# Which engines read the late copy of the test's sum, and which queue stores two of the last row blocks

## The chip, the cores and the metric

The kernel runs on one core of a Trainium2 chip. The metric is the device time of one execution in microseconds. The core has five engines with a sequencer each: TensorE (PE; its weight loads are shown as PEld), VectorE (DVE), ScalarE (ACT), GpSimd (POOL) and SyncE (SP). A sequencer issues its engine's instructions in their order, waits on semaphores, branches, and can issue DMAs. In this kernel SyncE, ScalarE and GpSimd issue DMAs, each on a queue of its own.

## The reference

An attention with a sliding window of 128 keys and 4 "sink" keys is followed by a gated block with a residual. All is float32; B = 4, H = 8, S = 768, D = 64, so rows of 512.

```python
scores = scale * np.matmul(q, k.transpose(0, 1, 3, 2))
keep = is_sink | in_window
scores = np.where(keep, scores, -1000000000.0)
scores = scores - np.max(scores, axis=-1, keepdims=True)
a = np.exp(scores)
a = a / (np.sum(a, axis=-1, keepdims=True) + 1e-09)
x = np.matmul(a, v)                      # heads joined to (4, 768, 512)
...
h = gelu_tanh(x @ w_in)                  # 512 -> 1024, split into u and v
v_n = (v - mu) / np.sqrt(var + 1e-06) * g_ln
v_s = np.einsum('ts,bsd->btd', w_sg, v_n) + b_sg[None, :, None]
return x + (u * v_s) @ w_out
```

## The kernel before, in words

The kernel works on 16 pairs of heads (4 batches of 4 pairs) and, per batch, on one block of the gated part. For a pair it loads k, q and v, brings k and q to columns, computes the scores only where the window or the sinks let through, takes exp without the maximum, multiplies by v with a column of ones for the denominator, and scales. For a batch it computes the two halves of the hidden layer, normalises v, multiplies by `w_sg`, gates, and projects with `w_out`. The result of a batch leaves in six blocks of 128 rows: a matmul group (`pj`), an addition of the residual on VectorE (`o`, line 918) and a store to the result (`store`, line 928).

Nothing is scheduled at run time. Every step is an `Op` with a name; a list of names, `FIRST`, gives the order in which all steps are written out, and so the order of each engine's own instructions. The buffers `o_sb` hold a row block from the addition until its store has landed.

The batch 3 blocks end the kernel. They are written in the order 2 (`pj32`), 1, 0, 3, 4, 5, and then a block of batch 2 in two halves of 256 columns, `pj23x` and `pj23y` (`LAST = (2, 3)`, chosen to come at the end). Stores go on SyncE's queue, but for the second half, `store23y`, which goes on ScalarE's.

Leaving out the maximum is right only while no denominator is out of range. So there is a test: GpSimd compares all reciprocals with two bounds (`compare`), TensorE adds up the ones (`tally`), VectorE reduces them to one integer, `total` (`summed`, lines 1112 and 1114). At the end, `with tc.If(found["total"] < COUNT)` (line 1306) branches: every engine compares the value in its own register, and when the sum is full it jumps over `general()`, a second, slow version of the whole computation. For this, every engine must load the sum from memory to a register (`ask`, line 1126, a TENSOR_LOAD in the profile).

Five engines do so at different places. SyncE loads `total` in the step `peek`, ScalarE in `peek_act`. VectorE, TensorE and GpSimd load a copy of it: the step `copied` (line 1140) writes `total` into the first column of the buffer of row block `MARK = (3, 4)`, which it may do only when that block's store has landed, since the store reads that buffer. The step `look` then loads from there. Behind the branch comes the end of the program (line 1338): GpSimd settles the semaphores of its own DMA queue, SyncE waits for all semaphores in turn, and a barrier joins the engines.

Of the kernel before, what the change touches and what calls it, by code (L numbers as in the profile page):

```python
# [9 lines left out]
I32 = mybir.dt.int32  # L10
# [39 lines left out]
class Planner:  # L50
# [15 lines left out]
    def add(self, *args, **kwargs):  # L66
        op = Op(*args, **kwargs)
        self.ops.append(op)
        return op
# [86 lines left out]
    "look"  # L156
)
TAKERS = (
    "zero_a0:ACT zero_a1:DVE zero_a2:DVE zero_a3:DVE low_a:DVE zero_b0:DVE zero_b1:DVE "
# [19 lines left out]
def kernel(  # L179
# [14 lines left out]
    nc = tc.nc  # L194

    B, H, S, Dh = q.shape
# [33 lines left out]
        o_sb=([128, DM], F32), st=([128, 6], F32))  # L230
# [5 lines left out]
    def bank(shape, dtype, name, buf=None):  # L236
        if buf is not None and buf.room is R["s"]:
            return ps_s.tile(shape, dtype, name=name, tag="s")
        return ps_m.tile(shape, dtype, name=name, tag="m")

    T = {}
    add = plan.add
# [10 lines left out]
    WARM = 8  # L253
    AHEAD = (0, 1)
    LAST = (2, 3)
    MARK = (B - 1, 4)
    LONG = ()
    BY_DMA = (11,12,13,14,15)
    W_DMA = ()
# [21 lines left out]
    total = consts.tile([128, 1], I32, name="total")  # L281
# [53 lines left out]
    def make_mask(m, at):  # L335
        for h in range(2):
# [6 lines left out]
                    rank=-2000)  # L343
    T["dark0"] = add("dark0", {"DVE": 450}, lambda _: make_dark0(), [T["dark"]], use=[dark],
                     rank=-1998)
# [5 lines left out]
    if LONG:  # L351
        T["spread"] = add("spread", {"POOL": 900}, lambda _: make_spread(), new=[spread],
                          rank=-378)
# [83 lines left out]
    def pos(n):  # L437
        return divmod(n, HP)
# [451 lines left out]
    def project(b, t, rank, rooms):  # L890
        ps = Buf([R[r] for r in rooms])
        o_sb = Buf([R["k_f"], R["q_f"], R["o_sb"]] if b == B - 1 else R["o_sb"])
        gT, x = T["gT", b], T["x", b]

        halves = [slice(0, DM)] if (b, t) != LAST else \
            [slice(0, DM // 2), slice(DM // 2, DM)]
        for i, cols in enumerate(halves):
            whole, w = len(halves) == 1, cols.stop - cols.start
            if i:
                ps = Buf([R[r] for r in rooms])  # L900
                o_sb = Buf(o_sb.rooms)
            tail = "" if whole else "xy"[i]

            def emit(_, ps=ps, cols=cols, w=w):
                ps.tile = bank([128, 512], F32, "o_ps", ps)
                for c in range(KU):
                    nc.tensor.matmul(ps.tile[:, 0:w], gT.tile[:, c, 128 * t:128 * (t + 1)],  # L907
                                     w_out_sb[:, c, cols], start=(c == 0), stop=(c == KU - 1))

            T["pj", b, t] = a = add(f"pj{b}{t}{tail}", {"PE": 865 if whole else 435}, emit,  # L910
                    [T["gT_", b, f, t // HT] for f in range(KU)] + [T["w_out"]],
                    new=[ps], use=[gT, x], rank=rank)

            def leave(_, ps=ps, o_sb=o_sb, cols=cols, w=w):
                tag = o_sb.room.name
                o_sb.tile = work.tile([128, DM], F32, name="o_sb", tag=tag, bufs=R[tag].size)
                heads = slice(cols.start // 128, cols.stop // 128)
                nc.vector.tensor_add(  # L918
                    o_sb.tile[:, 0:w].rearrange("p (h d) -> p h d", d=128),
                    ps.tile[:, 0:w].rearrange("p (h d) -> p h d", d=128),  # L920
                    x.tile[:, heads, t, :])

            a = add(f"o{b}{t}{tail}", {"DVE": 690 if whole else 380}, leave, [a], new=[o_sb],
                    use=[ps, x], rank=rank - 2000)

            def store(_, o_sb=o_sb, cols=cols, w=w, i=i):
                queue = nc.scalar if i else nc.sync
                queue.dma_start(out=out[b, 128 * t:128 * (t + 1), cols],
                                in_=o_sb.tile[:, 0:w])

            T["o_sb", b, t] = o_sb
            T["st", b, t] = add(f"store{b}{t}{tail}", {"ACT" if i else "SP": 380}, store, [a],
                                use=[o_sb], rank=-50, move=800 if whole else 400, lag=300)


# [76 lines left out]
    def turn_g(_):  # L1012
# [4 lines left out]
    a = add("turn_g", {"PE": 330}, turn_g, [T["g_row"], T["one"]], new=[g_ps], use=[g_row],  # L1017
            rank=9000)
# [20 lines left out]
    def block(b, rank, gate):  # L1039

        ahead = [T[("sc", *g)] for g in gate]
        gate = [T[("exp", *g)] for g in gate]
        cols = [T["xc", HP * b + hp] for hp in range(HP)] + ahead
        got = [hidden_v(b, j, rank + 0.1 * j, cols, gate) for j in range(NT)]
        for m in range(2):
            normalise(b, list(range(HT * m, HT * (m + 1))), rank + 0.05)
        got += [hidden_u(b, f, m, rank + 1 + 0.1 * f + m, cols, gate)
                for m in range(2) for f in range(KU)]
        rooms = ["m", "s"] if b == B - 1 else ["m"]
        for m in range(2):  # L1050
            for f in range(KU):
                spatial(b, f, m, 10000 + 1000 * b + 10 * (KU * m + f), rooms)
        for t in range(NT):
            project(b, t, 10500 + 1000 * b + 10 * t, rooms)
        return got

    gate = []
    for n in range(NP):
        r = 100 * n
        b, hp = pos(n)  # L1060
# [25 lines left out]
    COUNT = 2 * 128 * NP * NT * 2  # L1086
    flat = rcps.rearrange("p n c i h o -> p (n c i h o)")

    def compare(_):
# [8 lines left out]
    a = add("compare", {"POOL": 900}, compare,  # L1098
            [T["rcp", n, c] for n in range(NP) for c in range(2)],
            new=[fits], rank=12000)  # L1100
# [8 lines left out]
    a = add("tally", {"PE": 180}, tally, [a], new=[ps], use=[fits], rank=12900)  # L1109
# [6 lines left out]
    a = add("summed", {"DVE": 500}, summed, [a], use=[ps], rank=12900)  # L1116
    found = {}
# [2 lines left out]
              mybir.EngineType.SP]  # L1120

    WHY = "a sum of so many zeros and ones"
    ASKED = [mybir.EngineType.SP, mybir.EngineType.Activation]

    def ask(tile, engines):
        return nc.values_load(tile[0:1, 0:1], engines=engines, min_val=0, max_val=COUNT,
                              skip_runtime_bounds_check_because=WHY)

    def peek(_):
        found["SP"] = ask(total, ASKED[0:1])

    def peek_act(_):
        found["ACT"] = ask(total, ASKED[1:2])

    held_o = T["o_sb", *MARK]

# [2 lines left out]

    def look(_):
        tc.mark_branch_hint_location("rest", HINT, engines=HINTED)
        rest = ask(held_o.tile[:, 0:1].bitcast(I32), [e for e in mybir.ALL_ENGINES if e not in ASKED])
        found["total"] = type(rest).of_register_unchecked(
            type(rest.val)([*found["SP"].val, *found["ACT"].val, *rest.val]), min_val=0,
            max_val=COUNT)

    for part in segments:
        for lead, follow in zip(part[0::2], part[1::2]):  # L1150
# [2 lines left out]
            follow.rank = plan.first.get(follow.name, -10000)  # L1153
    for t in range(NT):
        T["pj", B - 1, t].behind.append(a)
    add("peek", {"SP": 750}, peek, [a], rank=0)
    add("peek_act", {"ACT": 750}, peek_act, [a], rank=0)
    T["st", -1, 0] = add("copied", {"DVE": 150}, copied, [a, T["st", *MARK]], use=[held_o],
                         rank=0)
    add("look", {"SP": 1200}, look, [a, T["st", -1, 0]] + [T["st", B - 1, t] for t in range(NT)], rank=0)  # L1160
    plan.run()

# [180 lines left out]
```

## Time and profile before

| what | value |
|---|---|
| three runs | 162.88, 165.15, 162.61 us; median 162.88 |
| the profiled execution | 162.92 us |
| its span, first to last instruction | 160.9 us |
| granted TensorE clock, mean | 0.998 |
| busy: PE, DVE, ACT, POOL | 94%, 82%, 67%, 52% of the span |
| DMA | 32.42 MB, 201 GB/s over the span |
| read from HBM, written | 24.81 MB, 6.29 MB |

The profile is of one execution, whose own time of 162.92 us is 2.0 us more than its span: what comes before the first and after the last instruction belongs to an execution too. Times in the views count from the start of the span. Names are those of the program: `out_dram<-o_sb` is a store of a row block, `o_sb<-o_ps,x` the addition before it, `o_sb<-total` the late copy, `<-total` and `<-o_sb` at line 1126 the loads to a register. An engine's name with a q behind it (SPq, POOLq) is its sequencer, whose instructions don't count as busy. The view of one line lists, for each kind of instruction, how many there were, their minimum, median and maximum duration in ns, and the first and the last start in us.

### The profile page before, as it was taken

How to read it: one execution, taken by the hardware profiler on the slowest of the kernel's cores; microseconds unless marked ns; L12 is line 12 of the kernel's file. 1: busy time of each engine (PE TensorE's matmuls, PEld its weight loads, DVE VectorE, ACT ScalarE, POOL GpSimd, SP SyncE). 2: the span in 40 equal slices, each digit the busy share in tenths (PEclk: the TensorE clock that was granted, in tenths of full speed). 3: DMA queues.
4: the chain of work that ended last, by engine and by line, in shares of the span. 5: the costliest groups of instructions: out<-in, count | busy, mean ns of one | idle time of the engine just before them, and what ended most of it. 6: DMA issues, size and time to landing. Idle time of an engine off the chain costs nothing.

```text
span 160.9 us, 4016 instructions
## 1 busy us (share of the span) xinstructions
PE 151.2 (94%) x1562; PEld 87.7 (55%) x1562; DVE 132.3 (82%) x283; ACT 107.6 (67%) x143; POOL 83.5 (52%) x126
## 2 busy tenths in 40 slices
PE   6899999999999999999799999998999999999960
PEld 2454574667657576456555664545556545555530
DVE  7556887798897999789999989589999969888960
ACT  6198787897979797979686875747995187701100
POOL 3645944155899695287957743573779403200000
PEclk9999999999999999999999999999999999999999
DMA  4999999998999956999876879799966330130182
GB/s 152 332 247 311 194 169 201 203 304 265 344 306 295 275 143 182 328 238 259 141 218 154 194 188 257 131 297 256 215 172 175 114 130 0 65 134 0 65 322 82
DMA packets 67877, 32.42 MB, mean 201 GB/s; under 512 B 56564, under 2 KB 64772, under 8 KB 67856
## 3 DMA queue, kind: packets, MB, share of 16 engines
q1 hardware_dynamic: 65328, 29.26, 70.1%
q0 software_dynamic: 2384, 2.75, 10.6%
q8 instruction: 13, 0.21, 0.6%
q10 hardware_dynamic: 144, 0.13, 0.2%
q14 instruction: 8, 0.07, 0.1%
HBM read 24.81 MB, written 6.29 MB: 193 GB/s over the span
## 4 chain that ended last, share of the span: by engine, by line
PE 79%; DVE 8%; POOL 4%; DMA 4%; ACT 1%; issue 1%; SPq 0%; DVEq 0%; POOLq 0%; ACTq 0%
PE vs L864 20%; PE hv L751 11%; PE o_ps L907 11%; PE hu L793 10%; PE sc L610 9%; PE av L676 8%; PE cps L550 4%; PE sc L590 3%; DMA q_f<-in_q_dram 2%; DVE vn L840 2%; PE xps L726 2%; POOL mv L820 2%; DVE o_sb L918 2%; DMA out_dram<-o_sb 2%; DVE mv L826 1%; DVE ex L638 1%
## 5 line engine op out<-in xcount | busy, mean ns | idle before, releaser
L627 ACT ACTIVATE ex<-sc 128x1024 bf16<-128x1024 f32 x48 | 47.4, 1024 | 9.7 <-PE sc L610 9.6
L864 PE MATMUL vs<-wsgT,vn 128*128 128x384 bf16 x192 | 35.5, 326 | 1.4 <-DVE vn L840 1.1
L864 PEld LDWEIGHTS <-vn 128*128 128x128 bf16 x192 | 17.5, 98 | 13.1 <-DVE vn L840 1.5
L793 PE MATMUL hu<-xT,w_in_sb 128*128 128x384 bf16 x128 | 23.6, 326 | 0.8 <-DVE o_sb L918 0.8
L801 ACT ACTIVATE uT<-hu 128x384 bf16<-128x384 f32 x32 | 14.9, 489 | 12.3 <-PE hu L793 12.1
L907 PE MATMUL o_ps<-w_out_sb,gT 128*128 128x512 bf16 (+1 forms) x100 | 23.1, 371 | 0.0
L751 PE MATMUL hv<-w_in_sb,xT 128*128 128x512 bf16 x96 | 22.5, 379 | 0.0
L875 DVE SCALAR_TENSOR_TENSOR vs<-vs,g_sb,b_bc 128x384 f32<-128x384 f32 x32 | 19.6, 621 | 2.8 <-PE vs L864 1.2
L773 DVE BATCH_NORM_STATS2 st<-v_all 128x6 f32<-128x512 f32 x24 | 16.3, 677 | 6.3 <-ACT v_all L762 6.3
L249 POOL CAST cast<-k_f 128x768 bf16<-128x768 f32 x16 | 13.7, 858 | 14.1 <-DMA k_f<-in_k_dram 12.8
L610 PE MATMUL sc<-qT,kT 64*128 64x256 bf16 (+2 forms) x320 | 18.9, 249 | 0.4 <-ACT qT L247 0.4
L311 POOL TENSOR_SCALAR_AFFINE_SELECT ex<-ex 128x512 bf16<-128x512 bf16 (+1 forms) x23 | 15.1, 655 | 7.9 <-ACT ex L627 7.7
L676 PEld LDWEIGHTS <-ex 128*128 128x128 bf16 x480 | 16.7, 97 | 4.1 <-issue 1.4
L695 DVE TENSOR_TENSOR x<-av,rcps 128x384 bf16<-128x384 f32 x32 | 17.5, 552 | 0.9
L883 DVE TENSOR_TENSOR gT<-vs,uT 128x384 bf16<-128x384 f32 x32 | 17.5, 556 | 0.9
L676 PE MATMUL av<-v_sb,ex 128*128 128x65 bf16 x352 | 18.0, 194 | 0.1
L249 POOL CAST cast<-q_f 128x768 bf16<-128x768 f32 x15 | 13.1, 872 | 9.7 <-issue 4.6
L793 PEld LDWEIGHTS <-w_in_sb 128*128 128x128 bf16 x128 | 12.3, 98 | 9.7 <-issue 1.2
L918 DVE TENSOR_TENSOR o_sb<-o_ps,x 128x512 f32<-128x512 f32 (+1 forms) x25 | 16.2, 663 | 1.3 <-PE o_ps L907 1.2
L762 ACT ACTIVATE v_all<-hv 128x512 f32<-128x512 f32 x24 | 13.7, 598 | 5.2 <-PE hv L751 5.0
L249 POOL CAST v_sb<-v_f 128x768 bf16<-128x768 f32 x16 | 13.9, 869 | 2.3 <-DMA v_f<-in_v_dram 2.3
L751 PEld LDWEIGHTS <-xT 128*128 128x128 bf16 x96 | 9.2, 98 | 10.5 <-DVE xT L249 0.6
(71 smaller groups left out, 197.6 us busy)
## 6 DMA issues: line engine op xcount, KB each, us to landing
k_f<-in_k_dram SPq DMA_DIRECT2D x16, 384.0 KB, 5.9
q_f<-in_q_dram SPq DMA_DIRECT2D x16, 384.0 KB, 5.1
v_f<-in_v_dram SPq DMA_DIRECT2D x16, 384.0 KB, 5.9
out_dram<-o_sb SPq DMA_DIRECT2D x23, 256.0 KB, 2.2
wsg<-in_moe_w_sg_dram POOLq DMA_DIRECT2D x2, 576.0 KB, 10.5
w_in_sb<-in_moe_w_in_dram POOLq DMA_DIRECT2D x2, 512.0 KB, 7.6
w_out_sb<-in_moe_w_out_dram POOLq DMA_DIRECT2D x1, 512.0 KB, 7.8
b_bc<-in_moe_b_sg_dram SPq DMA_DIRECT2D x1, 384.0 KB
```

Of the source, the lines that this page charges most:

```text
L249: eng[e].tensor_copy(dst, src)
L610: nc.tensor.matmul(sc.tile[row:row + keys, h, col:col + m], kT.tile[rows, k0:k0 + keys], qT.tile[rows, q0:q0 + m], start=not by_pe, stop=n ...
L627: nc.scalar.activation(out=ex.tile, in_=sc.tile, func=AF.Exp, scale=scale)
L676: nc.tensor.matmul(av.tile[:, m, h, :], ex.tile[:, h, col:col + 128], val, start=first, stop=(m == HT - 1 and h == 1 and at == len(steps) ...
L695: nc.vector.tensor_mul(x.tile[:, hp, HT * c:HT * (c + 1), :].rearrange("p i (h d) -> p i h d", h=2), av.tile[:, :, :, 0:64], rcp.to_broadc ...
L751: nc.tensor.matmul(ps.tile[:, 0:512], xT.tile[:, c, 128 * j:128 * (j + 1)], w_in_sb[:, c, DF:], start=(c == 0), stop=(c == KD - 1))
L793: nc.tensor.matmul(ps.tile[:, 0:NH], w_in_sb[:, c, 128 * f:128 * (f + 1)], xT.tile[:, c, NH * m:NH * (m + 1)], start=(c == 0), stop=(c == ...
L864: nc.tensor.matmul(ps.tile[:, 0:NH], vn.tile[:, si, 128 * f:128 * (f + 1)], wsgT[:, si, cols], start=(si == 0), stop=(si == NT - 1))
L875: nc.vector.scalar_tensor_tensor(out=ps.tile[:, 0:NH], in0=ps.tile[:, 0:NH], scalar=g_sb[:, f:f + 1], in1=b_bc[:, cols], op0=ALU.mult, op1 ...
L883: nc.vector.tensor_mul(gT.tile[:, f, cols], ps.tile[:, 0:NH], uT.tile[:, f, cols])
L907: nc.tensor.matmul(ps.tile[:, 0:w], gT.tile[:, c, 128 * t:128 * (t + 1)], w_out_sb[:, c, cols], start=(c == 0), stop=(c == KU - 1))
L918: nc.vector.tensor_add(o_sb.tile[:, 0:w].rearrange("p (h d) -> p h d", d=128), ps.tile[:, 0:w].rearrange("p (h d) -> p h d", d=128), x.til ...
```

## The change

GpSimd and VectorE no longer load the late copy but `total` itself, in steps of their own, `peek_POOL` and `peek_DVE`. TensorE is the only engine left that loads the copy. The copy goes into the buffer of row block 3 in place of row block 4, and so it waits for that block's store. The stores of row blocks 3 and 5 of batch 3 go on ScalarE's queue. Line numbers of the changed kernel are up to three higher.

```diff
-    "gT301 hu331 gelu_u331 peek_act store32 gT331 pj31 o31 store31 pj30 o30 store30 pj33 o33 "
-    "store33 pj34 o34 store34 pj35 o35 store35 pj23x o23x store23x pj23y o23y store23y copied "
-    "look"
+    "gT301 hu331 gelu_u331 peek_POOL store32 gT331 pj31 o31 store31 pj30 o30 store30 pj33 "
+    "peek_ACT o33 store33 pj34 o34 store34 pj35 o35 store35 pj23x o23x store23x pj23y o23y "
+    "store23y peek_DVE copied look"
...
-    MARK = (B - 1, 4)
+    BY_ACT = {(B - 1, 3), (B - 1, 5)}
+    MARK = (B - 1, 3)
...
+            by = "ACT" if i or (b, t) in BY_ACT else "SP"
+
-            def store(_, o_sb=o_sb, cols=cols, w=w, i=i):
-                queue = nc.scalar if i else nc.sync
+            def store(_, o_sb=o_sb, cols=cols, w=w, by=by):
+                queue = nc.scalar if by == "ACT" else nc.sync
...
-    ASKED = [mybir.EngineType.SP, mybir.EngineType.Activation]
+    EARLY = dict(SP=mybir.EngineType.SP, ACT=mybir.EngineType.Activation,
+                 POOL=mybir.EngineType.Pool, DVE=mybir.EngineType.DVE)
...
-    def peek(_):
-        found["SP"] = ask(total, ASKED[0:1])
-
-    def peek_act(_):
-        found["ACT"] = ask(total, ASKED[1:2])
+    def peek(e):
+        found[e] = ask(total, [EARLY[e]])
...
-        rest = ask(held_o.tile[:, 0:1].bitcast(I32), [e for e in mybir.ALL_ENGINES if e not in ASKED])
+        rest = ask(held_o.tile[:, 0:1].bitcast(I32),
+                   [e for e in mybir.ALL_ENGINES if e not in EARLY.values()])
...
-    add("peek_act", {"ACT": 750}, peek_act, [a], rank=0)
+    for e in EARLY:
+        add("peek" if e == "SP" else f"peek_{e}", {e: 100 if e == "DVE" else 750}, peek, [a], rank=0)
```

On GpSimd, behind its last arithmetic (the second normalisation of batch 3), stood the load of the late copy; a name's number is that of its buffer, and `o_sb_2753` is row block 4:

```order
L818 TENSOR_SCALAR mv_2497<-mv_2497 128x3 [waits DVE_49]
L820 TENSOR_TENSOR mv_2497<-mv_2497,half_72 128x3 [waits Pool_49]
L818 TENSOR_SCALAR mv_2497<-mv_2497 128x3 [waits DVE_49]
L820 TENSOR_TENSOR mv_2497<-mv_2497,half_72 128x3 [waits Pool_49]
L1126 TENSOR_LOAD o_sb_2753 [waits DVE_49]
L1306 COMPARE_AND_BRANCH
```

Now the load at the same place takes `total`:

```order
L819 TENSOR_SCALAR mv_2497<-mv_2497 128x3 [waits DVE_49]
L821 TENSOR_TENSOR mv_2497<-mv_2497,half_72 128x3 [waits Pool_49]
L819 TENSOR_SCALAR mv_2497<-mv_2497 128x3 [waits DVE_49]
L821 TENSOR_TENSOR mv_2497<-mv_2497,half_72 128x3 [waits Pool_49]
L1130 TENSOR_LOAD total_90 [waits DVE_49]
L1308 COMPARE_AND_BRANCH
```

The wait is for VectorE both times: before for the late copy, now for `total`. On VectorE, the end of the program before was this; `o_sb_2745`, `_2753` and `_2761` are row blocks 3, 4 and 5, `_2769` and `_2777` the two halves, and a wait on DMAHW is one for the landing of a DMA:

```order
L918 TENSOR_TENSOR o_sb_2753<-o_ps_2748,x_2132 128x512 [waits DMAHW6_49,PE_49]
L918 TENSOR_TENSOR o_sb_2761<-o_ps_2756,x_2132 128x512 [waits DMAHW7_49,DVE_49,PE_49]
L918 TENSOR_TENSOR o_sb_2769<-o_ps_2764,x_1545 128x256 [waits DMAHW2_49,PE_49]
L918 TENSOR_TENSOR o_sb_2777<-o_ps_2772,x_1545 128x256 [waits DMAHW3_49,PE_49]
L1140 COPY o_sb_2753<-total_90 128x1 [waits DMAHW2_49,DVE_49]
L1126 TENSOR_LOAD o_sb_2753 [waits DVE_49]
L1306 COMPARE_AND_BRANCH
```

Now it is this, with row block 3 in `o_sb_2748`:

```order
L919 TENSOR_TENSOR o_sb_2756<-o_ps_2751,x_2132 128x512 [waits DMAHW6_49,PE_49]
L919 TENSOR_TENSOR o_sb_2764<-o_ps_2759,x_2132 128x512 [waits DMAHW7_49,DVE_49,PE_49]
L919 TENSOR_TENSOR o_sb_2772<-o_ps_2767,x_1545 128x256 [waits DMAHW2_49,PE_49]
L919 TENSOR_TENSOR o_sb_2780<-o_ps_2775,x_1545 128x256 [waits DMAHW3_49,PE_49]
L1130 TENSOR_LOAD total_90 [waits DVE_49]
L1141 COPY o_sb_2748<-total_90 128x1 [waits DMAHW1_49,DVE_49]
L1308 COMPARE_AND_BRANCH
```

VectorE's load moved ahead of the copy, and the copy waits for another store. On ScalarE, the end before was:

```order
L801 ACTIVATE uT_2542<-hu_2672 128x384 [waits PE_49]
L801 ACTIVATE uT_2542<-hu_2713 128x384 [waits PE_49]
L1126 TENSOR_LOAD total_90 [waits DVE_49]
L928 DMA out_0_dram<-o_sb_2777 128x256 [waits DMAHW4_49,DVE_49]
L1306 COMPARE_AND_BRANCH
```

And now:

```order
L802 ACTIVATE uT_2542<-hu_2713 128x384 [waits PE_49]
L1130 TENSOR_LOAD total_90 [waits DVE_49]
L931 DMA out_0_dram<-o_sb_2748 128x512 [waits DMAHW1_49,DVE_49]
L931 DMA out_0_dram<-o_sb_2764 128x512 [waits DMAHW3_49,DVE_49]
L931 DMA out_0_dram<-o_sb_2780 128x256 [waits DMAHW5_49,DVE_49]
L1308 COMPARE_AND_BRANCH
```

Row blocks 3 and 5 came onto ScalarE's queue ahead of the last half, and left SyncE's. Each store there stands behind a wait for its addition and for an earlier DMA. TensorE's order is the same as before, but for the buffer that its load reads. No other instruction of the path past the branch is moved.

More of the change, by code (lines that the diff above doesn't have):

```diff
@@ L931, in project @@
             T["o_sb", b, t] = o_sb
-            T["st", b, t] = add(f"store{b}{t}{tail}", {"ACT" if i else "SP": 380}, store, [a],
+            T["st", b, t] = add(f"store{b}{t}{tail}", {by: 380}, store, [a],
                                 use=[o_sb], rank=-50, move=800 if whole else 400, lag=300)
@@ L1143, in look @@
         tc.mark_branch_hint_location("rest", HINT, engines=HINTED)
-        rest = ask(held_o.tile[:, 0:1].bitcast(I32), [e for e in mybir.ALL_ENGINES if e not in ASKED])
-        found["total"] = type(rest).of_register_unchecked(
-            type(rest.val)([*found["SP"].val, *found["ACT"].val, *rest.val]), min_val=0,
-            max_val=COUNT)
+        rest = ask(held_o.tile[:, 0:1].bitcast(I32),
+                   [e for e in mybir.ALL_ENGINES if e not in EARLY.values()])
+        regs = [r for e in EARLY for r in found[e].val] + list(rest.val)
+        found["total"] = type(rest).of_register_unchecked(type(rest.val)(regs), min_val=0,
+                                                          max_val=COUNT)
     for part in segments:
@@ L1155 @@
         T["pj", B - 1, t].behind.append(a)
-    add("peek", {"SP": 750}, peek, [a], rank=0)
-    add("peek_act", {"ACT": 750}, peek_act, [a], rank=0)
+    for e in EARLY:
+        add("peek" if e == "SP" else f"peek_{e}", {e: 100 if e == "DVE" else 750}, peek, [a], rank=0)
     T["st", -1, 0] = add("copied", {"DVE": 150}, copied, [a, T["st", *MARK]], use=[held_o],
```

## The prediction, made before the run

> **What bounds the kernel now.** I read the page first: its busy shares, and TensorE's row of the 40 slices, of 4.0 us each.
>
> ```profile
> span 160.9 us, 4016 instructions
> PE 151.2 (94%) x1562; PEld 87.7 (55%) x1562; DVE 132.3 (82%) x283; ACT 107.6 (67%) x143; POOL 83.5 (52%) x126
> PE   6899999999999999999799999998999999999960
> ```
>
> TensorE is at work in nearly every slice, so up to about 156 us it sets the time. The change touches no matmul and nothing that a matmul waits for; it lies in the last two digits, 6 and 0. So I turned to the end of the chain of waits, and to the busy time of all engines in three stretches of the tail (their columns: length, then busy time of PE, PEld, DVE, ACT and POOL, the clock, the share of the DMA engines, GB/s).
>
> ```profile
> 150.33 3.47 PE o_ps L907 x16
> 153.82 0.70 DVE o_sb L918
> 154.54 2.72 DMA out_dram<-o_sb
> 157.35 0.15 DVE o_sb L1140
> ...
> 156.10:157.30 1.20, 0.00 (x0) 0.00 (x0) 0.00 (x0) 0.00 (x0) 0.00 (x0) 1.00 0.92 337
> 157.30:158.10 0.80, 0.00 (x0) 0.00 (x0) 0.15 (x1) 0.00 (x0) 0.00 (x0) 1.00 0.54 175
> 158.10:160.90 2.80, 0.00 (x0) 0.00 (x0) 0.00 (x0) 0.00 (x0) 0.00 (x0) 0.91 0.04 12
> ```
>
> From 156.1 to 160.9 no engine computes, but for one copy of 0.15 us: 4.8 us of ending. The chain says what they hang on: the store of row block 4, which lands 2.72 us after 154.54, then the copy of the sum at 157.35. The chain stops at the last busy instruction. What fills the other 3.4 us are the sequencers' own instructions, which the view of one source line shows: the reads of the sum (L1126), the branch past the general code (L1306), the end of the program (L1338). In each row, after the minimum, median and maximum duration, stand the first and the last start.
>
> ```profile
> L1126 SPq TENSOR_LOAD <-total x1: 517/517/517, 141.3 to 141.3; - x1
> L1126 ACTq TENSOR_LOAD <-total x1: 713/713/713, 150.4 to 150.4; - x1
> L1126 POOLq TENSOR_LOAD <-o_sb x1: 487/487/487, 157.5 to 157.5; - x1
> L1126 DVEq TENSOR_LOAD <-o_sb x1: 542/542/542, 157.5 to 157.5; - x1
> L1126 PEldq TENSOR_LOAD <-o_sb x1: 487/487/487, 157.5 to 157.5; - x1
> ...
> L1306 POOLq EVENT_SEMAPHORE  x5: 17/43/43, 158.6 to 158.9; - x5
> L1306 SPq COMPARE_BRANCH  x1: 67/67/67, 156.3 to 156.3; - x1
> L1306 ACTq COMPARE_BRANCH  x1: 68/68/68, 156.5 to 156.5; - x1
> L1306 ACTq EVENT_SEMAPHORE  x1: 17/17/17, 157.0 to 157.0; - x1
> L1306 POOLq COMPARE_BRANCH  x1: 45/45/45, 158.1 to 158.1; - x1
> L1306 PEldq EVENT_SEMAPHORE  x1: 51/51/51, 158.6 to 158.6; - x1
> L1306 DVEq EVENT_SEMAPHORE  x1: 21/21/21, 158.8 to 158.8; - x1
> L1306 POOLq INC_SWDGE_SEM  x1: 292/292/292, 159.0 to 159.0; - x1
> ...
> SPq L1338 <- DMA w_out_sb<-in_moe_w_out_dram: 2.9, 1, 2.9
> ...
> L1338 SPq EVENT_SEMAPHORE  x12: 28/28/28, 159.3 to 160.0; - x12
> ```
>
> SyncE branches at 156.3 and then waits 2.9 us at the end of the program. The weight transfer that the list of waits names as its releaser is not to be taken for it: that is the "landed long ago" case. What happens when the wait ends is POOL's INC_SWDGE_SEM at 159.0, 292 ns long; PE and DVE had done their last step at 158.6 and 158.8. So the end runs: landing of row block 4, copy (157.35), POOL's read (157.5), POOL's branch (158.1), five waits (158.6 to 158.9), INC_SWDGE_SEM (159.0), then SyncE's twelve waits, 0.06 us apart, from 159.3 to 160.0, and the barrier to 160.9. GpSimd's reading of the late copy bounds the end.
>
> Beside it runs a shorter path, the last stores themselves (start, duration, then who; last, the median time from issue to landing of the two half stores, and the least, median and greatest of the stores from 130 us on).
>
> ```profile
> 153.68 0.33 SPq L928 DMA_DIRECT2D out_dram<-o_sb  x1
> 155.40 0.33 SPq L928 DMA_DIRECT2D out_dram<-o_sb  x1
> 155.62 0.41 DVE L918 TENSOR_TENSOR o_sb<-o_ps,x 128x256 f32<-128x256 f32 x1
> 155.83 0.39 SPq L928 DMA_DIRECT2D out_dram<-o_sb  x1
> 156.07 0.39 ACTq L928 DMA_DIRECT2D out_dram<-o_sb  x1
> ...
> out_dram<-o_sb SPq DMA_DIRECT2D x1, 128.0 KB, 2.4
> out_dram<-o_sb ACTq DMA_DIRECT2D x1, 128.0 KB, 2.5
> ...
> DMA to landing us min/median/max: 2.0/2.2/2.5
> ```
>
> The very last store leaves ScalarE's queue at 156.07 and lands 2.5 us later (158.53 in the trace's record); the half before it lands at 155.83 + 2.4 = 158.2.
>
> **The change, part by part.**
>
> *GpSimd reads the sum early.* Its last work ends at 136.97 + 0.89 = 137.9 and the sum is written at 137.6 + 0.15:
>
> ```profile
> 136.97 0.89 POOL L820 TENSOR_TENSOR mv<-mv,half 128x3 f32<-128x3 f32 x1
> L1114 DVE CAST total<-count x1: 154/154/154, 137.6 to 137.6; 128x1 int32<-128x1 f32 x1
> ```
>
> Its read, branch, waits and INC_SWDGE_SEM then run near 138 to 140, under 16 us of TensorE's work. It queues nothing behind them but the end barrier. This takes the 157.35-to-159.3 piece off the path. Cost: nothing while that cover stands; uncovered, it is what it was.
>
> *VectorE reads early, in its own order.* The read (0.54) now stands between the last addition (155.62 + 0.41 = 156.04) and the copy. ScalarE's read at 150.4 ran beside its activation, so the cost lies between 0 and 0.54: VectorE reaches the copy at 156.0 to 156.6.
>
> *The mark moves from row block 4 to 3.* The copy now waits for a store issued at 153.68. With the least landing of 2.0 and the chain's 2.72 as ends, it lands at 155.7 to 156.4. The copy starts at the later of the two, 156.0 to 156.6, against 157.35 before. Behind it wait VectorE's own branch and TensorE's read. From the copy's start to TensorE's last step took 158.65 - 157.35 = 1.3, so TensorE is done at 157.3 to 157.9. I take 157.5, nearer the low end, because ScalarE's case is the one shown.
>
> *Two stores move from SP's queue to ScalarE's.* Blocks 3 and 5: two issues of 0.33 leave SyncE, two join ScalarE, whose queue is empty from the read's end at 151.1 to 156.07. ScalarE's earlier issue at 155.40 would end near 155.8, before 156.07, so the last half is not held up. On SyncE, the other half now waits for its data alone and leaves some 0.09 us earlier. The amount stored is the same, and in 156.1 to 157.3 the DMA engines are 0.92 busy, so I expect the last landing where it was: 158.53, between 156.07 + 2.0 = 158.1 (the least time) and 159.2 (below).
>
> *The sum.* SyncE branches at about 156.3. ScalarE needed 0.5 from its branch to its next step (156.5 to 157.0); by that SyncE starts its twelve waits at 156.8 and would pass them by 157.5. TensorE is ready by then or by 157.9, so what stops SyncE is the last store at 158.53. In the trace's records the ninth wait, at 159.3 + 8 x 0.06 = 159.77, is the one on that store's semaphore; from there to the end it took 160.91 - 159.77 = 1.14. (Were it the first, 1.6; the last, 0.9.) So the new span is 158.53 + 0.03 + 1.14 = 159.7, less by 1.2. The profiled run took 162.92 us, 2.0 more than its span; the median of the runs is 162.88, the same to 0.04. The forecast is 162.9 - 1.2 = **161.7 us**, 0.7% less.
>
> **The rivals.**
>
> *Instruction fetches beside the last stores.* The page lists code transfers as a kind of their own among the DMA queues:
>
> ```profile
> q8 instruction: 13, 0.21, 0.6%
> q14 instruction: 8, 0.07, 0.1%
> ```
>
> VectorE and TensorE now branch near 156.5 and 157.0, while the last halves are under way. If a branch brings a fetch that delays one DMA engine, the store lands late by what the slowest store of the chain has over the least: 2.72 - 2.0 = 0.7. Then the landing is 159.2, the span 160.4 and the time 162.4. Against it: SyncE and ScalarE branched in the same 156.3 to 157.0 before. The Trainium skill has it as a rule ("Runtime: NRT & Kernel Launch", Instruction fetch mechanics): a taken branch to code outside the loaded window costs a DMA fetch before execution goes on. By that rule POOL's 0.5 us from branch (158.1) to next step (158.6) would be such a stall and the time could go to the 162.4 above; the trace shows the gap, not its cause.
>
> *Two queues land sooner.* If stores on two queues overlap better, the last half lands in the least time, at 158.1, and the time is 161.2. The 0.92 share speaks against it. So does the Trainium skill ("DMA: Bandwidth & Descriptors", Issuing engines are not separate DMA queues): all queues share the same 16 DMA engines, and a second issuer saves issue time alone. By that rule the stores are worth the 0.09 us of issue, which my sum leaves out.
>
> *The end was not POOL's.* If something that stays released SyncE at 159.3, nothing is gained: 162.9. For it speaks only that the list of waits names another releaser.
>
> *Slower: the mark's store is late on ScalarE's queue.* TensorE still waits for it. If it lands as slowly as the loads of the page,
>
> ```profile
> k_f<-in_k_dram SPq DMA_DIRECT2D x16, 384.0 KB, 5.9
> ```
>
> at 153.68 + 5.9 = 159.6, TensorE is done at 160.9 and with 0.9 to come the span is 161.8, the time 163.8. It decides from a copy at 160.9 - 0.9 - 1.3 = 158.7 on, that is a landing after 5.0 us; no store of the tail took over 2.72.
>
> **How the numbers follow.** Forecast 0.68, fetches 0.16, sooner landing 0.07, no gain 0.06, slower 0.03. The range runs from the sooner landing, 161.2, to the fetch case, 162.4, each with 0.1 more for the scatter of runs: 161.1 to 162.5. That holds 0.91 by the cases; I leave it so, since the run of 165.15 among three shows that a median can stray. A difference of 2%, 3.3 us here, is about what a measurement of this kernel can tell from no change; no case reaches it, so within 2% has 0.96, and 0.02 each is left for a faster and a slower time outside these cases.
>
> **What would show it.** In the profile of the changed kernel: POOL's read, branch and INC_SWDGE_SEM near 138 to 140; VectorE's read near 156; the copy at 156.0 to 156.6; TensorE's last step before 158; three stores on ScalarE's queue, the last at 156.1; SyncE's last waits split at about 158.5, where the last half store lands; span 159.7. The forecast is wrong if the last landing moves (the fetch case by up to 0.7), if TensorE's last step comes after the landing, or if SyncE's first wait still ends near 159.3.

## The result, and the profile after

Over 20 runs of each, beside each other, the changed kernel took 162.00 us (median; 160.56 to 165.60) and the kernel before 162.69 us (161.82 to 165.15), so the medians are 0.69 us apart. The ratio is 0.9947, 95% interval 0.9922 to 0.9973, which is 0.86 us less (0.44 to 1.27). Medians here and below are of all runs, while the ratios leave out the runs over 1.5% above the fastest of their kernel, the profiled one of the changed kernel (163.09 us) among them. The forecast was 161.7 us, in a range of 161.1 to 162.5. In a second series, twelve runs of the changed kernel had a median of 161.88 us, a ratio of 0.9949 (0.992 to 0.9979).

The profiled run took 163.09 us, with a span of 161.1 us, longer than the 160.9 before. That is no contradiction, but a warning about single profiles:

```profile
span 161.1 us, 4001 instructions
PE 150.2 (93%) x1547; PEld 87.2 (54%) x1562; DVE 131.2 (81%) x283; ACT 107.5 (67%) x143; POOL 83.5 (52%) x126
PE   6879999998899999999979999999999999999990
```

TensorE's row is as full as before; only its last digits, 9 and 0 for 6 and 0, show that the work ended later. In the profiles of all kernels of this study the end of the last addition lies anywhere from 154.6 to 157.3 us, whatever was changed behind it; in this one it was 157.22, in the one of before 156.04. So all that follows is counted **from the end of the last addition**, and the "tail" is the time from there to the end of the span. The tail was 160.91 - 156.04 = 4.87 us before and 161.12 - 157.22 = 3.90 us after.

The reads of the sum, the branch and the end of the program in the changed kernel (duration in ns, then first and last start):

```profile
L1130 POOLq TENSOR_LOAD <-total x1: 486/486/486, 138.9 to 138.9; - x1
L1130 ACTq TENSOR_LOAD <-total x1: 713/713/713, 151.6 to 151.6; - x1
L1130 DVEq TENSOR_LOAD <-total x1: 543/543/543, 156.8 to 156.8; - x1
L1130 PEldq TENSOR_LOAD <-o_sb x1: 772/772/772, 157.7 to 157.7; - x1
...
L1308 POOLq COMPARE_BRANCH  x1: 45/45/45, 139.5 to 139.5; - x1
L1308 POOLq INC_SWDGE_SEM  x1: 296/296/296, 140.4 to 140.4; - x1
L1308 SPq COMPARE_BRANCH  x1: 67/67/67, 157.3 to 157.3; - x1
L1308 DVEq COMPARE_BRANCH  x1: 84/84/84, 157.5 to 157.5; - x1
...
L1308 PEldq COMPARE_BRANCH  x1: 388/388/388, 158.5 to 158.5; - x1
L1308 DVEq EVENT_SEMAPHORE  x1: 21/21/21, 158.6 to 158.6; - x1
L1308 PEldq EVENT_SEMAPHORE  x1: 51/51/51, 159.0 to 159.0; - x1
...
L1340 SPq EVENT_SEMAPHORE  x6: 28/28/28, 157.5 to 157.8; - x6
...
L1340 SPq EVENT_SEMAPHORE  x4: 27/28/28, 158.6 to 160.0; - x4
```

GpSimd's INC_SWDGE_SEM is over by 140.7, VectorE reads beside its last addition, and TensorE's last step is at 159.0. VectorE needs 1.1 us from its branch (157.5) to its next step (158.6), where it needed 0.6 in the kernel before; as TensorE's last step and the last landing come later, that costs nothing here. SyncE's first six end waits pass in one go from 157.5; the next four, in the last row, are spread over 158.6 to 160.0. The list of waits names what ends them (us in total, times, the longest):

```profile
SPq L1340 <- DMA out_dram<-o_sb: 2.0, 4, 0.7
```

Before, the same list named one wait of 2.9 us for a transfer that had landed long ago, the mark of a wait that was really for GpSimd. Now it names the output stores, four times. The copy of the sum, and the issue of the last half store (start, duration):

```profile
157.46 0.15 DVE L1141 COPY o_sb<-total 128x1 int32<-128x1 int32 x1 [0.23 <-DVE o_sb L919]
157.26 0.34 ACTq L931 DMA_DIRECT2D out_dram<-o_sb  x1
...
DMA to landing us min/median/max: 2.6/2.7/2.8
```

The copy starts 0.23 us after the last addition (before: 1.32). The last half store, issued at 157.26, needs 2.8 us; it lands at 160.02 in the trace's record, SyncE's wait for it passes at 160.04, and the span ends 1.10 us after the landing. The last landing bounds the end now, as forecast.

### The profile page after: what moved, and what is told of

It reads as the page before. It is cut to its first block, busy times and chain, and to the rows that moved or that the text cites. A ratio compares the mean times of both kernels' runs of the same rounds, so it can differ in the third digit from the quotient of the medians.

```text
span 161.1 us, 4001 instructions
## 1 busy us (share of the span) xinstructions
PE 150.2 (93%) x1547; PEld 87.2 (54%) x1562; DVE 131.2 (81%) x283; ACT 107.5 (67%) x143; POOL 83.5 (52%) x126
## 5 line engine op out<-in xcount | busy, mean ns | idle before, releaser
L908 PE MATMUL o_ps<-w_out_sb,gT 128*128 128x512 bf16 (+1 forms) x91 | 22.6, 370 | 0.5
```

## The experiments

Two theories were put against each other first. **The later of two**: the end follows whichever comes last, the chain of a late read (GpSimd's read, branch and INC_SWDGE_SEM above all), or the landing of the last store. Its rivals: each part brings a share of its own, or the stores on ScalarE's queue bring some of it. The mark alone raised a second question, a stall behind GpSimd's branch, and the profile of after a third, why the last store lands late. All numbers of this table but the times are from the profiles, in us after the end of the last addition; "INC" is the start of GpSimd's INC_SWDGE_SEM (a negative one came long before).

| kernel | time, median | ratio to before (95%) | copy | INC | last landing | tail |
|---|---|---|---|---|---|---|
| before | 162.69 | - | 1.32 | 2.98 | 2.49 | 4.87 |
| after | 162.00 | 0.9922 to 0.9973 | 0.23 | -16.85 | 2.80 | 3.90 |
| after, again (g3) | 161.88 | 0.992 to 0.9979 | 0.23 | -16.84 | 3.22 | 4.31 |
| GpSimd's read alone (e1) | 161.91 | 0.9895 to 0.9964 | 1.42 | -16.85 | 2.53 | 3.94 |
| all but GpSimd's read (e2) | 161.81 | 0.9937 to 1.0018 | 0.23 | 2.15 | 2.92 | 4.05 |
| mark alone (e3) | 164.58 | 1.0049 to 1.0154 | -0.09 | 5.05 | 2.64 | 6.95 |
| stores alone (e4) | 162.67 | 0.9967 to 1.0031 | 1.48 | 3.11 | 2.64 | 5.01 |
| mark, 24 empty instructions (f1) | 164.86 | 1.0094 to 1.0195 | -0.08 | 5.10 | 2.47 | 6.99 |
| before, one empty instruction (f2) | 164.57 | 1.0095 to 1.0184 | 1.34 | 5.16 | 2.55 | 7.05 |
| mark, GpSimd hinted (g1) | 162.12 | 0.9896 to 0.9973 | -0.08 | 1.90 | 3.02 | 4.16 |
| mark, 64 empty instructions (g4) | 161.49 | 0.9917 to 0.9972 | -0.08 | 1.82 | 3.22 | 4.38 |
| before, VectorE shifted (g2) | 162.27 | 0.9958 to 1.0014 | 0.59 | 2.48 | 2.05 | 4.38 |
| after, VectorE shifted (f3) | 160.72 | 0.984 to 0.9933 | 0.24 | -16.84 | 2.17 | 3.27 |
| after, fewer stores (f4) | 160.80 | 0.985 to 0.9927 | 0.23 | -16.84 | 1.99 | 3.20 |

### GpSimd's early read alone (e1)

Against the changed kernel:

```diff
-    EARLY = dict(SP=..., ACT=..., POOL=..., DVE=...)
+    EARLY = dict(SP=..., ACT=..., POOL=...)
-    BY_ACT = {(B - 1, 3), (B - 1, 5)}
-    MARK = (B - 1, 3)
+    BY_ACT = set()
+    MARK = (B - 1, 4)
```

> The kernel before with one part of the change: only GpSimd reads the sum itself early; VectorE and TensorE still read the late copy, the copy waits for row block 4, all stores as before. I measure the tail, from the end of the last addition to the end of the span: 4.87 us before, 3.90 us with the whole change. Theory A (the end is the later of two paths: the late readers, and the landing of the last store plus some 1.1 us): GpSimd's path is gone, next are VectorE's last step, 1.4 us after the copy's start, and the last landing, nearly at the same time; tail 3.7 to 4.0, time 0.9 to 1.1 us below the kernel before. Theory B (the parts of the change add up, each a share): tail between the two, about 4.4, half the gain. Theory C (the stores on two queues made the gain): tail 4.8 to 4.9, no gain.

It took 161.91 us, a ratio of 0.9929, and its tail is 3.94, as short as that of the whole change. The copy is as late as before (1.42), so VectorE's late read is the next in line, and SyncE's list of waits names it:

```profile
SPq L1339 <- DVEq L1129: 1.4, 1, 1.4
SPq L1339 <- PEq L1339: 0.7, 2, 0.5
SPq L1339 <- DVEq L1307: 0.3, 1, 0.3
...
SPq L1339 <- DMA out_dram<-o_sb: 0.2, 1, 0.2
```

VectorE's last step is at 2.84 in this kernel, behind the last landing at 2.53; the end comes 1.10 after the former. GpSimd alone had held the end back.

### All but GpSimd's read (e2)

```diff
-    EARLY = dict(SP=..., ACT=..., POOL=..., DVE=...)
+    EARLY = dict(SP=..., ACT=..., DVE=...)
```

> The whole change but for one part: GpSimd reads the late copy again, as TensorE does. Theory A: the copy now starts 0.2 us after the last addition in place of 1.3, so GpSimd's path (1.9 us from the copy's start to SyncE's first end wait) is over by 2.2 us after the last addition, before the last store lands at 2.5 to 2.8; tail 3.7 to 4.0, as with the whole change. My prediction on record named GpSimd's early read as what takes its path away; if A holds, that part was not needed beside the new mark. Theory B: without its largest part the change loses half its gain or more, tail 4.4 or longer.

161.81 us, a ratio of 0.9977 whose interval takes in 1; the tail, 4.05, is within 0.15 of after's. SyncE's first end wait is again the long one:

```profile
SPq L1339 <- DMA w_out_sb<-in_moe_w_out_dram: 2.2, 1, 2.2
```

That is the sign of GpSimd. But with the mark on row block 3 its copy comes 1.09 us earlier, its INC at 2.15 for 2.98, and from INC to the end it takes 1.90 us, as in every kernel in which GpSimd is last (1.89 to 1.90 in before, e3, e4, f1, f2 and g2). INC gains less than the copy because GpSimd's read, now just behind the last addition, took 0.77 us for 0.49. 2.15 + 1.90 = 4.05, just above the 3.7 to 4.0 expected; the landing alone would give 2.92 + 1.10 = 4.02. So the parts don't add up: GpSimd's early read without the mark (e1), and the mark without GpSimd's early read (e2), each bring nearly the whole gain in the tail, and either makes the other worth little. By the runs' times that is shown for e1; the interval of e2 takes in no gain as well as the whole one.

### The stores alone (e4)

```diff
-    EARLY = dict(SP=..., ACT=..., POOL=..., DVE=...)
+    EARLY = dict(SP=..., ACT=...)
-    MARK = (B - 1, 3)
+    MARK = (B - 1, 4)
```

> The kernel before with one part alone: the stores of row blocks 3 and 5 leave on ScalarE's queue; readers and mark (block 4) as before. Theory A: the copy still waits for block 4's landing, GpSimd's path still ends last; tail 4.7 to 5.0, no gain. Theory C: a good part of the gain, tail 4.0 to 4.4, with block 4 or the last half landing sooner than 2.4 us after its issue.

162.67 us against 162.76, a ratio of 0.9999 (0.9967 to 1.0031), tail 5.01. Two stores on the other queue are worth nothing that these runs can show: the first half leaves at -0.30 for -0.21, 0.09 earlier, as forecast, and its landing hides that.

### The mark alone (e3): a stall

Against the kernel before:

```diff
-    MARK = (B - 1, 4)
+    MARK = (B - 1, 3)
```

> The kernel before with one part alone: the late copy goes to the buffer of row block 3 in place of 4; readers and stores as before. Theory A: the store of block 3 on SyncE's queue lands before the last addition ends, the copy starts within 0.1 us of that, GpSimd's path frees SyncE 1.9 to 2.0 us after the last addition, the last store lands at 2.5 to 2.8; tail 3.7 to 4.0, one number changed gives the whole gain. Theory B: a share, tail 4.3 to 4.7. Theory C: none, 4.8 to 4.9.

It is slower: 164.58 us, a ratio of 1.0101 (1.0049 to 1.0154). The copy is indeed early, at -0.09, and GpSimd branches at 156.5. But then this:

```profile
L1307 POOLq EVENT_SEMAPHORE  x5: 17/43/43, 160.2 to 160.5; - x5
L1307 POOLq COMPARE_BRANCH  x1: 45/45/45, 156.5 to 156.5; - x1
L1307 POOLq INC_SWDGE_SEM  x1: 300/300/300, 160.6 to 160.6; - x1
```

From the branch to GpSimd's next step pass 3.7 us; in the kernel before it was 0.5 (158.1 to 158.6). In the built program nothing on GpSimd's path had changed, but the general code, over which GpSimd jumps, had 141 instructions in place of 140. New theory: GpSimd's branch stalls when its target lies too far on in the code, in blocks that are loaded piece by piece. Rival: the early copy makes something else late.

### One empty instruction on GpSimd in the kernel before (f2)

Against the kernel before:

```diff
+        for _ in range(1):
+            nc.gpsimd.engine_nop()
         nc.gpsimd.memset(ones, 1.0)
```

> The kernel before with one empty instruction more on GpSimd, ahead of its branch; nothing else. Theory D: the branch's target is at the same place as in the kernel with the mark alone, one instruction further than in the kernel before, and falls into the block that is not loaded; GpSimd stands some 3.2 us longer, tail 4.87 + 3.2 = 8.1, time near 166. Theory E: no effect, tail 4.7 to 5.0, time near 162.8.

164.57 us, a ratio of 1.014 (1.0095 to 1.0184): one empty instruction, run at 124.5 us under TensorE's work, costs 2.2 us of tail.

```profile
L1309 POOLq EVENT_SEMAPHORE  x5: 17/43/43, 160.4 to 160.8; - x5
L1309 POOLq COMPARE_BRANCH  x1: 45/45/45, 157.8 to 157.8; - x1
```

The stall (2.7 us here, so that the tail is 7.05 and not the 8.1 expected) needs no early copy. What changed is where GpSimd's code stands.

### Shifting the branch by 24, by 64, and a hint (f1, g4, g1)

Each against the mark-only kernel; in f1 the number is 24:

```diff
+        for _ in range(64):
+            nc.gpsimd.engine_nop()
         nc.gpsimd.memset(ones, 1.0)
```

> The kernel with the mark alone on row block 3, whose tail came out at 6.95 us in place of the 3.7 to 4.0 expected: GpSimd took 3.7 us from its branch to the next instruction, against 0.48 in the kernel before. In the built program the code that GpSimd jumps over is 141 instructions there and 140 in all others, since a wait behind the branch was split in two. Theory D (code layout: by that one instruction the branch's target falls into a block of code that is not loaded yet, and GpSimd stands until it is fetched; 8 KB is 128 instructions of 64 bytes): with 24 empty instructions on GpSimd ahead of the branch, the branch too moves to the next block, the target is the block after it and is loaded ahead; gap 0.4 to 0.6, tail 3.7 to 4.0, time near 161.8. Theory E (the stall belongs to the mark: three engines read and branch while the last stores are under way, and GpSimd's fetch is held up by them): gap 3 to 4 us again, tail near 6.9, time near 164.5.

Twenty-four changed nothing: 164.86 us, the gap 3.7 us again (157.4 to 161.1). So the cure by this shift failed. If the code comes in blocks, a shift too small to carry the branch over the next block's edge would change nothing; that was tried next.

> The third block's mark alone, with 64 empty instructions on GpSimd at the place where 24 changed nothing. Stall theory by position (the target lies more than one block of code behind the branch; 64 carry the branch over a block boundary, so that the next block is brought in on the way): a code transfer near 125 to 126 us, where the empty instructions run, gap 0.4 to 0.7 us, tail 3.7 to 4.1, time about 161.8. Rival (what costs is the longer jump itself, or anything about the empty instructions): gap 2.5 to 3.8, tail 5.8 to 7.0, time 163.9 to 164.9.

Sixty-four cured it: 161.49 us, and one code transfer, as expected, where the empty instructions run (the DMA queues of this kernel from 125.0 to 126.5 us; packets, MB, share):

```profile
L1309 POOLq EVENT_SEMAPHORE  x5: 17/42/43, 156.9 to 157.3; - x5
L1309 POOLq COMPARE_BRANCH  x1: 45/45/45, 156.5 to 156.5; - x1
...
q14 instruction: 1, 0.01, 2.1%
```

The gap is 0.5 us (0.47 in the trace's record). The other cure leaves the place alone and adds GpSimd to the engines that get the branch hint:

```diff
     HINTED = [mybir.EngineType.PE, mybir.EngineType.Activation, mybir.EngineType.DVE,
-              mybir.EngineType.SP]
+              mybir.EngineType.SP, mybir.EngineType.Pool]
```

> The third block's mark alone (as in the mark-only kernel, whose tail after the last addition was 6.95 us with 3.7 us between GpSimd's branch and its next step), and GpSimd added to the engines that get the branch hint, which the other four have. Stall theory (GpSimd waits for code at the branch's target, and a hint lets that code be brought in beforehand): a code transfer of 8192 bytes shows on GpSimd's account well before its branch, the gap falls from 3.7 to 0.4 to 0.7 us, the tail to 3.7 to 4.1, the time to about 161.8. Rival (the gap isn't code, or a hint doesn't fetch on GpSimd): gap 2.5 to 3.8, tail 5.8 to 7.0, time 163.9 to 164.8.

```profile
L1307 POOLq EVENT_SEMAPHORE  x5: 17/43/43, 158.1 to 158.5; - x5
L1307 POOLq COMPARE_BRANCH  x1: 65/65/65, 157.6 to 157.6; - x1
```

The gap is 0.5, the time 162.12, a ratio of 0.9934. The early code transfer that the expectation asked for doesn't show, though; and since the hint is itself one more instruction, this run alone would not tell the hint from the shift by one. The shift by 24 that failed makes the hint the likelier. With the stall gone both kernels end with the last landing (3.02 + 1.14, 3.22 + 1.16). Their tails, 4.16 and 4.38, are above the 3.7 to 4.1 expected, because that landing came late; by the runs' times the mark alone brings what the whole change brings, as the later-of-two theory has it.

By the count of instructions, the branch's target stands one place further on than in the kernel before in e3 and in f2, 25 in f1 and 65 in g4: the first three stall, the last does not. In g1 it is two places, with the hint, and there is no stall.

What stays open is what GpSimd waits for in the stall. It ends at 4.63, 4.74 and 4.68 us after the last addition in e3, f2 and f1, though the branches came at 0.94, 2.08 and 0.94, so it isn't a fixed time from the branch, and the code transfers in it can't be told from those that the kernel before has at about the same times. That it depends on the place of the code is shown; the fetch itself isn't.

### Fewer stores at the end (f4)

```diff
             def store(_, o_sb=o_sb, cols=cols, w=w, by=by):
+                if i:
+                    return
```

> The changed kernel without the store of the last half block (256 columns of 128 rows of the result are left out); its matmuls and addition stay. Theory A (the last landing bounds the end): the end now follows the landing of the half before, 0.3 to 0.5 us earlier; tail 3.4 to 3.6. If something else stands close behind the landing, as TensorE's late read with its last step 1.75 us after the last addition: TensorE would give 1.75 + some 1.0 = 2.8 at the earliest, so it does not show here. Tail 3.8 to 4.0 would say that the landing is not the bound.

This kernel leaves out both halves of row block 3 of batch 2, not the last alone as the expectation has it: `i` is read when the store is written out, after the loop has ended. Its last store is that of row block 5, which lands at 1.99, and the tail is 3.20, 1.21 after it (the time 160.80); four of SyncE's waits, 0.06 us apart, stand behind that landing, where two stood behind the last one in after. TensorE's last step, at 1.47, came before it. The landing bound is confirmed, by another store than meant; the numbers expected for the last half can't be compared.

### Why the last store lands late (f3, g2, g3)

In the profile of after, 15 of the 16 increments of the last store's semaphore are in by 2.06 us after the last addition, and the sixteenth by 2.80. Before, it was 2.05 and 2.49. So one of the 16 parts of a store is late, in each of the last four stores; I take it for one late DMA engine of the 16, though the trace doesn't name the engine. In every profile with such a straggler, an instruction transfer of 8 KB starts 0.4 to 0.7 us ahead of the last addition's end. The queues from 155.3 to 156.0 in before, and then from 156.7 to 157.3 in after:

```profile
q1 hardware_dynamic: 115, 0.23, 85.2%
q14 instruction: 1, 0.01, 5.0%
```

```profile
q1 hardware_dynamic: 112, 0.21, 92.2%
q14 instruction: 1, 0.01, 3.4%
```

Theory: it is VectorE's code, brought in as VectorE moves on through its program, and it holds one engine. Then empty instructions at VectorE's start should shift it. Against after (f3) and against before (g2):

```diff
         nc.vector.memset(half, -0.5)
+        for _ in range(40):
+            nc.vector.engine_nop()
```

> The changed kernel with 40 empty instructions on VectorE near its start. In the profile of the changed kernel the last store ends on one of its 16 DMA engines 0.7 us after the 15 others (15 done 2.06 us after the last addition, the last at 2.80), and so do the two stores before it; stores ahead of an 8 KB instruction fetch of 0.3 to 0.6 us, that starts 0.46 us before the last addition ends, have no such straggler. Theory F (that fetch is VectorE's, on crossing a block of its code near its end, and it holds one DMA engine up): 40 instructions more let VectorE cross the block some 20 us earlier; no fetch there, stragglers of under 0.3, last landing 2.1 to 2.4 after the last addition, tail 3.2 to 3.6. Theory G (the fetch is another engine's, or the straggler has another cause): tail 3.8 to 4.1.

Three transfers of after, at 27.6, 92.2 and 156.8 us, stand at 8.1, 77.1 and 130.0 in f3, while those at 43.7, 55.1 and 140.6 stay, at 43.5, 54.3 and 139.4; from 155.3 to 156.3 the queues show none. The last store's fifteenth and sixteenth increments come at 2.09 and 2.17. Landing times from 153 us on, and SyncE's waits for the stores:

```profile
DMA to landing us min/median/max: 2.1/2.1/2.1
...
SPq L1341 <- DMA out_dram<-o_sb: 0.8, 3, 0.4
```

The tail is 3.27 and the time 160.72 us, a ratio of 0.9887 (0.984 to 0.9933): the quickest complete kernel here, clearly ahead of before. Against after (0.9949, 0.992 to 0.9979, in another series) the intervals overlap by a little.

> The kernel before with 40 empty instructions at VectorE's start and nothing else, which in the changed kernel moved VectorE's code transfers away from the last stores. Theory (the late one of 16 DMA engines is held by VectorE's code transfer, in the kernel before at 155.40 us, upon row block 4's store): row block 4's store lands at 0.4 to 0.6 us after the last addition instead of 1.23, the copy follows at 0.5 to 0.7, and the tail is 4.1 to 4.4 instead of 4.87: about 162.1 us. Rival (the gain of the 40 in the changed kernel was chance, or belongs to its other store order): copy at 1.2 to 1.4, tail 4.8 to 5.0, time 162.7.

In the kernel before, the same shift lets row block 4 land at 0.50 for 1.23, so the copy comes at 0.59 for 1.32 and, with a read by GpSimd of 0.74 us for 0.49, INC at 2.48 for 2.98: tail 4.38, 0.49 less. The landing is all in by 2.05, but GpSimd still holds the end. The time, 162.27 us (0.9958 to 1.0014), is lower by 0.3 and not told apart from no change.

> The changed kernel itself once more, beside the others on one chip and for a second profile. If the straggling engine is a fixture of its code layout: a code transfer within 0.8 us ahead of the last addition's end, the last store's fifteenth completion at 2.0 to 2.2 and its last at 2.5 to 2.9 us after that addition, tail 3.6 to 4.0, time 161.6 to 162.0 against 160.7 for the kernel with the 40 empty instructions. If it was chance in one profile: last at 2.1 to 2.2, tail 3.2 to 3.4.

The changed kernel a second time, in a profile with a span of 160.0 us:

```profile
DMA to landing us min/median/max: 3.1/3.1/3.2
...
SPq L1340 <- DMA out_dram<-o_sb: 2.4, 4, 0.9
```

The straggler is there again, and larger: fifteenth at 2.06, sixteenth at 3.22, with a code transfer from 0.59 us ahead of the last addition's end. Its landing and its tail of 4.31 are beyond the 2.9 and 4.0 expected. So the straggler is a fixture of the code's layout, whose size differs from profile to profile: with the transfer the last store lands at 2.47 to 3.22 (eleven profiles), without it at 2.05 and 2.17.

## Why the prediction was right, point by point

- **What bounded the kernel before.** Right. GpSimd's chain: from its INC_SWDGE_SEM to the end it is 1.89 to 1.90 us in all seven kernels in which it is last, and taking it away alone (e1) took 0.93 off the tail.
- **GpSimd's early read at no cost.** Right: 138.9 to 140.7.
- **VectorE's read between 0 and 0.54.** Right, near the low end, as chosen: of its 0.54 all but 0.07 lay beside the addition, and the copy began at 0.23.
- **The mark's store.** Right. Issued at -2.36 and landed at -0.26, 2.1 us later, within the forecast's 2.0 to 2.72, so that the rival of a late mark fell. TensorE's last step was done 1.57 after the copy's start, not 1.3, since its read took 0.77 in place of 0.49. That is 1.80 after the last addition, at the high end of the stated 1.3 to 1.9 and not near the low end as chosen. It was still a microsecond ahead of the last landing.
- **The stores on ScalarE's queue.** Right: 0.09 of issue and nothing at the end (e4).
- **From the last landing to the end.** Right: 1.10 for the forecast's 1.17. The wait on that store is now the tenth of SyncE's twelve, not the ninth, which is one wait of 0.06 less behind it.
- **The last landing unmoved.** This is the term that was mis-sized. The sum had it at 2.46 us after its issue, as in the profile of before; it took 2.77 in the profile of after and 3.19 in the second. That is the shortfall in the profiles: a tail shorter by 0.97 and by 0.56, for a forecast of 1.2. By runs the time is shorter by 0.86, with an interval that still takes in 1.2. The value of before was near the low end of what such a kernel shows (2.47 to 3.22 after the last addition); the one sign of it in that profile was the 0.44 us between the fifteenth and the sixteenth increment. That the forecast came within 0.3 us of 162.00 is in part luck: the base taken from three runs, 162.88, was 0.19 above the median of twenty, and made up for a part of the shortfall.
- **What a measurement can tell.** Too coarse: 2% was taken as about the least difference that can be told from no change, and twenty runs of each gave an interval of 0.5% in width, so that the 0.5% found is clear of no change.
- **The rival of instruction fetches** had the kind right and the source wrong. A code transfer does make one part of the last stores late: against before, the last landing moved by 0.31 us in the profile of after and by 0.73 in the second, for the rival's 0.7. But the transfer was there before as well, so the rival put its whole price on top of a landing that already held 0.44 of such a delay; and it is VectorE's sequential code, not the code behind a branch. The Trainium skill ("Runtime: NRT & Kernel Launch", Instruction fetch mechanics) calls the cost of crossing a block of code mostly hidden; here it wasn't, 0.6 us of tail between after and f3, since it fell on the stores that end the kernel. By the Trainium skill (same page and section) a taken branch to a target outside the loaded window forces a fetch before execution goes on. A stall that comes and goes with the code's place, as in e3, f1, f2 and g4, fits that rule; but no run here shows the fetch, and a fetch of fixed length doesn't explain why the three stalls ended within 0.11 us of one another when one branch came 1.1 us after the other two.
- **Left out of the working:** that the parts would not add up (e1, e2), and that the mark moved alone would have cost 1%. The whole change shows no stall on GpSimd (its branch at 139.5, its next step at 140.0), and 16 us of TensorE's work would have covered one there. VectorE's branch did take longer in four of the five profiles in which VectorE reads early: 1.11 to 1.29 us to its next step in after, g3, e2 and f4, for 0.61 in before. In the fifth, f3, whose VectorE code is shifted, it took 0.60. VectorE was done ahead of the last landing in all of them, so nothing was lost by it; its cause stays open.

## What to carry to other kernels

The end of a kernel like this one is the later of a few chains, so take away the last one, price the gain against the next one, and don't add up the parts: here either half of the change took nearly the whole off the tail. Before a landing from a single profile goes into a sum, look at when 15 of its 16 increments were in; if the last one straggles, the landing will scatter, and a code transfer near it is the first suspect. A change to the order of an engine's instructions also moves its code, so a part that is "free" should be run once with a few empty instructions added: one of them was worth 1.4% here.

## What the runs showed of the hardware

- A branch on GpSimd over 140 or 141 instructions took 0.5 us to its next step in some layouts and 2.7 to 3.7 us in others; one empty instruction made the difference one way, 64 the other, 24 made none.
- With an 8 KB instruction transfer of 0.31 to 0.66 us ahead of the last store, the sixteenth increment of that store came 0.41 to 1.17 us after the fifteenth (eleven profiles), not in step with the transfer's own length: 0.74 us for one of 0.32 in after, 0.44 for one of 0.56 in before. The fifteenth didn't change (2.04 to 2.07, and 2.09 in f3). Two transfers that began at 1.57 and 1.62 in f3, with the last store already under way, left only 0.08 between the two.
- A read of the sum from memory to a register took 0.74 to 0.81 us where it began 0.1 to 0.8 us after the last addition (f4 apart), and 0.48 to 0.55 where it began at 1.5 to 1.7. The last stores seem to be the reason: TensorE's, begun at 0.43, took 0.772 us in after and 0.488 in f4, where the two half stores are left out. But VectorE's, begun at -0.47 with three stores under way, took 0.54, so not every store lengthens a read.
